# Blockwise attention and a cosine feed-forward on one core: where the last blocks' weight differences are split, the banks of the last block, and an early table load

## The chip, the cores and the metric

The kernel runs on one core of a Trainium2 chip. The metric is device microseconds of an execution. TensorE (PE) multiplies, and PEld in the profile is its loading of weights; VectorE (DVE), ScalarE (ACT) and GpSimd (POOL) compute; SyncE (SP) issues all transfers, in one fixed order.

## The reference

```
q, k, v: (8, 8, 576, 64) float32;  w_in: (512, 2048);  w_out: (2048, 512)
for every head and every chunk of 64 positions:
    s = q_c @ k_c.T / 8;  s = s - max(s);  a = exp(s);  a = a / (sum(a) + 1e-9);  out_c = a @ v_c
x = out, positions by heads: (4608, 512)
h = x @ w_in;  g = h * cos(h);  result = g @ w_out          # (4608, 512) float32
```

## The kernel before, in words

Tokens are worked in nine tiles of 512. Every large product is made in three passes of a rounded type (float32r): an operand is split into a high part (a rounding copy) and a low part (the operand less its high part), and high by high, high by low and low by high are summed in one bank of the accumulator memory. `copy_by` (L337) is the copy and `two_by` (L343) the subtraction; they run on the engine that the order names, so most splits of the whole kernel share the lines L339, L341 and L345. All matmuls have line 324 and all loads line 321.

The program does not issue its work directly. `piece` (L1076) records each step with its engine, an estimated length and what it waits for; at the end `in_order` (L283) issues all of them in the order of the list `RANK` (one place for each recorded piece), and the pieces in the list `ELSEWHERE` go to their other engine (ScalarE's copies to VectorE, VectorE's subtractions to GpSimd). On each engine and on SyncE the work runs strictly in that order. A reader can't see from the list which piece is where, so the places that matter are told in words below.

The start: `early` (L1137) makes the scores of four head pairs of tile 0; the first pair's maximum is negated and its exponentials are made chunk by chunk (L514), for the others the maximum is subtracted first (L506) and the exponential follows (L578). VectorE takes the maxima (L502), sums (L594) and inverses (L598, L599).

The middle: from tile 3 on, tiles go in pairs (a "unit"). The hidden layer of two tiles is made with seven products of half blocks instead of eight, named A11, S3, S2, A12, A22, S1, S4, whose weight operands (`combo`) were stored in the device's main memory (HBM) and are streamed in four rooms. Two of the units also make differences of w_out's blocks, `differences_of_w` (L1684): for each of eight pairs of row blocks it forms four differences V1 to V4, splits them into high and low parts on chip, and stores both parts in `diffs`.

The last unit: `last_pair` (L1781) makes the hidden layer of the last two tiles for eight pairs k. In a pair, the product S4 needs two adds on VectorE (`add_c`, `add_b`), which need the copy of S3's bank (`copy_d`). After S4 comes a chain of integer part (L972), turn (L975), sine (L979), product (L982), rounding copy and low part, before the pair's own block products. Sums of g's quarters (Z1 to Z4 and Z22) go to `sums` in HBM. Then `last_blocks` (L1911) makes the remaining products of the output layer: Z1 by V1, Z2 by V2, Z3 by V3, Z4 by a quarter of w_out itself, Z22 by V4, each in four groups kk, for tile i = 0 and 1. For each group it loads the difference (`w_load`), loads two sums into a room of a ring (`g_load`), splits the sums (`parts_of_g`), and multiplies (`block_part`). A sub-block of 128 by 256 of one group is six matmuls of 256 columns. Results are copied out of the banks X, Y, Z into the rows A to D, added to, and stored by `store_block`.

```
ring: K_ROOMS[0][0], K_ROOMS[1][0] (pair 6's), K_ROOMS[0][1], K_ROOMS[1][1] (pair 7's), two rooms of x
```

Of the kernel before, what the change touches and what calls it, by code (L numbers as in the profile page):

```python
# [20 lines left out]
P = 128  # L21
# [70 lines left out]
    35, 32, 38, 44, 48, 41, 16, 56, 60, 65, 66, 54, 72, 79, 81, 78, 74, 84, 90, 94, 87, 82, 93, 96, 98, 97, 101,  # L92
    110, 113, 116, 107, 109, 114, 120, 126, 131, 115, 135, 137, 142, 134, 123, 138, 147, 150, 149, 144, 162, 171,
    177, 156, 146, 159, 165, 168, 188, 180, 196, 200, 203, 193, 178, 201, 209, 214, 216, 227, 231, 237, 240, 222,
    233, 248, 250, 253, 262, 244, 266, 271, 273, 265, 257, 268, 270, 278, 277, 267, 280, 285, 287, 282, 288, 297,
    321, 328, 305, 300, 310, 316, 324, 331, 327, 335, 338, 344, 336, 322, 341, 351, 354, 347, 339, 353, 355, 356,
    362, 352, 365, 367, 368, 366, 364, 377, 380, 385, 378, 384, 388, 390, 397, 394, 386, 402, 406, 413, 403, 400,
    405, 412, 417, 420, 416, 422, 430, 441, 421, 409, 425, 438, 448, 447, 435, 453, 457, 460, 455, 442, 458, 462,
    467, 0, 14, 1, 2, 3, 4, 5, 7, 8, 11, 6, 12, 17, 20, 9, 19, 24, 27, 15, 26, 30, 10, 13, 22, 25, 28, 31, 36, 42,
    18, 23, 34, 39, 46, 45, 49, 29, 37, 43, 50, 53, 52, 59, 40, 47, 55, 63, 69, 61, 68, 51, 58, 62, 70, 75, 71,  # L100
    77, 21, 33, 64, 163, 92, 100, 105, 173, 95, 130, 172, 175, 111, 133, 186, 191, 179, 176, 205, 197, 183, 187,
    192, 211, 215, 219, 198, 207, 199, 204, 213, 221, 220, 224, 226, 228, 236, 241, 234, 238, 246, 255, 259, 252,
    256, 57, 67, 73, 80, 85, 88, 91, 99, 103, 106, 76, 83, 86, 89, 104, 108, 112, 117, 125, 127, 102, 119, 122,
    128, 136, 140, 148, 132, 129, 118, 124, 121, 141, 145, 151, 154, 167, 169, 143, 155, 158, 139, 152, 153, 157,
    160, 174, 182, 194, 170, 161, 166, 181, 164, 184, 190, 195, 208, 223, 225, 189, 202, 185, 210, 206, 212, 217,
    230, 245, 249, 260, 218, 243, 232, 229, 239, 235, 242, 247, 263, 269, 276, 264, 307, 258, 254, 251, 261, 274,
    283, 286, 289, 295, 299, 284, 279, 275, 272, 281, 291, 293, 296, 301, 304, 309, 302, 290, 294, 292, 298, 320,
    475, 308, 477, 314, 317, 303, 306, 535, 312, 313, 315, 318, 325, 329, 311, 332, 330, 319, 340, 333, 342, 346,
    349, 357, 360, 350, 334, 326, 323, 337, 359, 363, 369, 372, 375, 383, 361, 343, 348, 358, 345, 371, 374, 381,
    387, 398, 401, 382, 373, 370, 379, 376, 391, 395, 404, 407, 410, 414, 399, 389, 396, 424, 393, 419, 423, 428,  # L110
    432, 444, 449, 440, 450, 464, 446, 468, 470, 486, 491, 483, 493, 499, 507, 511, 518, 521, 528, 529, 542, 583,
    554, 545, 547, 561, 563, 568, 574, 548, 552, 565, 567, 576, 582, 586, 591, 609, 607, 601, 608, 612, 621, 625,
    629, 590, 597, 604, 619, 623, 627, 633, 660, 642, 649, 418, 415, 427, 411, 408, 426, 429, 433, 436, 439, 443,
    445, 437, 434, 451, 431, 452, 461, 465, 471, 480, 490, 466, 485, 454, 482, 463, 473, 481, 484, 488, 492, 494,
    487, 498, 513, 456, 459, 497, 503, 508, 515, 520, 526, 500, 495, 502, 512, 517, 504, 510, 514, 524, 527, 536,
    525, 519, 509, 506, 522, 531, 537, 539, 550, 553, 556, 530, 569, 558, 540, 546, 541, 559, 562, 566, 578, 581,
    560, 555, 551, 549, 544, 570, 572, 575, 585, 598, 602, 580, 573, 599, 577, 571, 587, 588, 595, 605, 630, 634,
    610, 606, 589, 603, 596, 615, 626, 628, 632, 635, 641, 624, 618, 617, 622, 614, 646, 648, 639, 644, 640, 643,
    638, 645, 647, 653, 656, 661, 668, 671, 637, 654, 657, 665, 667, 658, 664, 666, 669, 672, 676, 670, 681, 659,
    652, 663, 680, 684, 686, 688, 696, 701, 685, 697, 678, 694, 683, 692, 703, 705, 708, 714, 719, 702, 734, 691,  # L120
    722, 731, 712, 715, 720, 723, 738, 751, 713, 748, 753, 729, 711, 724, 730, 733, 737, 757, 760, 725, 392, 479,
    476, 478, 474, 533, 592, 532, 469, 472, 489, 496, 534, 501, 505, 516, 523, 593, 538, 543, 557, 564, 594, 579,
    584, 600, 611, 613, 616, 620, 631, 636, 651, 655, 662, 674, 677, 689, 693, 706, 650, 728, 690, 699, 726, 750,
    727, 673, 675, 679, 704, 687, 739, 700, 732, 695, 710, 716, 721, 709, 717, 682, 698, 707, 735, 743, 766, 740,
    747, 741, 745, 718, 772, 779, 778, 785, 820, 947, 857, 916, 834, 933, 986, 997, 1008, 764, 809, 842, 825, 758,
    815, 811, 762, 771, 783, 829, 791, 824, 831, 839, 902, 946, 777, 884, 943, 736, 742, 744, 746, 752, 770, 763,
# [2264 lines left out]
```

## Time and profile before

| | us |
|---|---|
| median of 3 runs (lowest, highest) | 782.38 (779.45, 783.24) |
| the profiled execution | 779.57 |
| its span, first to last instruction | 777.8 |
| PE busy in the span | 763.4 |
| DVE / ACT / POOL busy | 637.9 / 442.8 / 256.5 |

The granted clock of TensorE is 0.999 of full speed over the span. 184.59 MB move on the queue of the kernel's transfers. Times in the rows count from the span's start.

### The profile page before, as it was taken

To read this page: it belongs to the slowest core of one execution; us is meant where nothing else is said; L and a number is where in the kernel's file an instruction comes from. 1 tells how busy PE (TensorE), PEld (TensorE's weight loads), DVE (VectorE), ACT (ScalarE), POOL (GpSimd) and SP (SyncE) were. 2 spreads that over 40 slices of the span, in tenths; PEclk is the share of its full clock that TensorE was granted. 3 is DMA by queue.
4 is the path that set the end of the run, shared out by engine and by line. 5 is a ranking of instruction groups with operands and counts; after the bars stand their busy time and mean duration, and the time that the engine had idled before them with its cause. 6 is when DMAs were issued, how large, how long until landed. Compare 5 with 4: busy or idle time off the path is not lost.

```text
span 777.8 us, 16133 instructions
## 1 busy us (share of the span) xinstructions
PE 763.4 (98%) x6100; PEld 675.5 (87%) x6100; DVE 637.9 (82%) x1120; ACT 442.8 (57%) x811; POOL 256.5 (33%) x241
## 2 busy tenths in 40 slices
PE   7999999999999999999999999999999999999997
PEld 6888888888999988888888888888888889888997
DVE  5997889988999988987887878987788676688664
ACT  5998887366874547555644256454625366556222
POOL 2344125665443145341102345222123243433011
PEclk9999999999999999999999999999999999999999
DMA  9991922099959655897636737668743457999994
GB/s 336 409 419 44 350 83 82 23 333 329 340 188 303 210 195 204 266 316 234 215 108 236 254 114 267 214 217 305 244 139 123 162 173 253 295 284 376 374 382 148
DMA packets 100109, 185.61 MB, mean 239 GB/s; under 512 B 9408, under 2 KB 44224, under 8 KB 100032
## 3 DMA queue, kind: packets, MB, share of 16 engines
q1 hardware_dynamic: 100032, 184.59, 68.3%
q8 instruction: 48, 0.79, 0.4%
q14 instruction: 29, 0.24, 0.1%
HBM read 132.12 MB, written 52.43 MB: 237 GB/s over the span
## 4 chain that ended last, share of the span: by engine, by line
PE 88%; DVE 5%; DMA 3%; ACT 2%; issue 1%; SPq 1%; POOL 0%; ACTq 0%; DVEq 0%; POOLq 0%
PE acc L324 43%; PE h L324 33%; PE a L324 12%; DMA w_in<-combo 1%; DMA kt<-in_kT_dram 1%; DMA diffs<-w_in 1%; SPq L321 1%; DMA w_in<-sums 1%; DVE w_in L975 0%; DVE w_in L982 0%; ACT g_hi L341 0%; PE a L1202 0%; DVE g_lo L345 0%; DVE w_in L345 0%; ACT e L514 0%
## 5 line engine op out<-in xcount | busy, mean ns | idle before, releaser
L324 PE MATMUL acc<-w_out,g_hi 128*128 128x512 f32 (+1 forms) x992 | 281.6, 368 | 0.3 <-DVE g_hi L339 0.2
L324 PE MATMUL h<-x,w_in 128*128 128x512 f32 (+1 forms) x960 | 226.0, 364 | 0.2 <-DVE g L725 0.2
L324 PEld LDWEIGHTS acc<-w_out,g_hi 128*128 128x128 f32 x992 | 180.8, 189 | 23.9 <-DVE g_hi L339 0.4
L324 PEld LDWEIGHTS h<-x,w_in 128*128 128x128 f32 x960 | 170.9, 189 | 22.7 <-DVE x L687 0.5
L324 PE MATMUL acc<-w_out,g_lo 128*128 128x512 f32 (+1 forms) x496 | 181.5, 366 | 0.9 <-DVE g_lo L345 0.9
L345 POOL TENSOR_TENSOR g_lo<-g,g_hi 128x512 fp32r<-128x512 f32 x41 | 57.3, 1397 | 155.6 <-DVE g_hi L339 60.0
L324 PEld LDWEIGHTS acc<-w_out,g_lo 128*128 128x128 f32 x496 | 93.9, 189 | 12.9 <-DVE g_lo L345 1.3
L324 PE MATMUL h<-w_in,w_in 128*128 128x512 f32 (+1 forms) x384 | 98.3, 354 | 1.1 <-DMA w_in<-combo 0.9
L324 PEld LDWEIGHTS h<-w_in,w_in 128*128 128x128 f32 x384 | 65.8, 190 | 10.1 <-issue 1.0
L341 ACT CAST g_hi<-w_in 128x512 fp32r<-128x512 f32 x46 | 28.4, 619 | 54.3 <-PE acc L324 28.9
L345 DVE TENSOR_TENSOR g_lo<-w_in,g_hi 128x512 fp32r<-128x512 f32 x56 | 38.3, 689 | 18.8 <-ACT g_hi L341 16.7
L979 ACT ACTIVATE w_in<-w_in 128x512 f32<-128x512 f32 x64 | 39.3, 627 | 22.9 <-DVE w_in L975 22.8
L345 POOL TENSOR_TENSOR g_lo<-w_in,g_hi 128x512 fp32r<-128x512 f32 x16 | 20.9, 1310 | 63.4 <-DVE g_hi L339 30.3
L324 PE MATMUL a<-x,w_in 128*128 128x512 f32 (+1 forms) x192 | 41.1, 353 | 0.4 <-ACT g_hi L341 0.4
L324 PE MATMUL a<-w_in,w_in 128*128 128x512 f32 (+1 forms) x192 | 41.0, 353 | 0.0
L972 ACT ACTIVATE w_in<-w_in 128x512 int32<-128x512 f32 x32 | 20.1, 628 | 31.2 <-DVE w_in L969 25.8
L341 ACT CAST g_hi<-g 128x512 fp32r<-128x512 f32 x44 | 27.1, 618 | 18.1 <-PE acc L324 12.4
L324 PEld LDWEIGHTS a<-x,w_in 128*128 128x128 f32 x192 | 32.9, 190 | 4.6 <-ACT g_hi L341 0.7
L324 PEld LDWEIGHTS a<-w_in,w_in 128*128 128x128 f32 x192 | 32.9, 190 | 3.9
L966 ACT COPY a<-h 128x512 f32<-128x512 f32 x28 | 16.0, 573 | 33.7 <-PE h L324 33.6
L975 DVE SCALAR_TENSOR_TENSOR w_in<-w_in,h 128x512 f32<-128x512 int32 x32 | 21.9, 683 | 15.8 <-ACT w_in L972 13.3
L345 DVE TENSOR_TENSOR g_lo<-g,g_hi 128x512 fp32r<-128x512 f32 x43 | 32.1, 749 | 1.3 <-ACT g_hi L341 0.8
(250 smaller groups left out, 1483.1 us busy)
## 6 DMA issues: line engine op xcount, KB each, us to landing
w_in<-combo SPq DMA_DIRECT2D x84, 512.0 KB, 5.2
combo<-w_in SPq DMA_DIRECT2D x56, 256.0 KB, 5.0
w_in<-combo SPq DMA_DIRECT2D x56, 256.0 KB, 5.2
w_in<-sums SPq DMA_DIRECT2D x40, 256.0 KB, 6.2
qt<-in_qT_dram SPq DMA_DIRECT2D x36, 256.0 KB, 5.3
kt<-in_kT_dram SPq DMA_DIRECT2D x36, 256.0 KB, 5.5
w_in<-in_w_in_dram SPq DMA_DIRECT2D x16, 512.0 KB, 9.5
w_out<-in_w_out_dram SPq DMA_DIRECT2D x16, 512.0 KB, 9.6
```

What stands on the lines that cost most here:

```text
L321: kept(nc.sync.dma_start(out=out, in_=in_))
L324: kept(nc.tensor.matmul(*args, **kw))
L341: kept(nc.scalar.copy(out=out, in_=in_))
L345: kept(eng.tensor_tensor(out, a, b, op=op))
L966: kept(nc.scalar.copy(out=out, in_=in_))
L972: kept(nc.scalar.activation(g.bitcast(I32), h, AF.Identity, bias=0.25, scale=0.5 / math.pi))
L975: kept(nc.vector.scalar_tensor_tensor(g, g.bitcast(I32), -2.0 * math.pi, h, op0=ALU.mult, op1=ALU.add))
L979: kept(nc.scalar.activation(g, g, AF.Sin, bias=0.5 * math.pi))
```

## The change

- `differences_of_w` no longer splits: it stores the four differences as they are, two stores a call instead of four, and `diffs` has half the size.
- `w_load` loads a difference (256 KB instead of 512) into the low half of a room, and then two new pieces split it there: `high` (ScalarE, or VectorE) and `low` (VectorE, or GpSimd).
- The rooms are others: the two tiles of exponentials and a pair of `vt` tiles first, then the four streaming rooms, then nine rooms of x. Three more rooms of x join the ring of g's split parts (`g_where`). The ring of loaded sums begins with the two g tiles, so every later group moves up one room.
- Tile 1's last product (Z22 by V4) goes into a bank "W" of its own for each half, the banks that Z had; row D takes a copy of X after P7, and each half of W is added to it on VectorE.
- `added_to` stores its two halves as two pieces with places of their own. The copies of C wait for those of B.
- A memset and one exponential of a 128 by 1 tile stand at the start of the program.

```diff
+    table = const.tile([P, 1], F32, name="table")
+    kept(nc.vector.memset(table, 0.0))
+    kept(nc.scalar.activation(table, table, AF.Exp))
...
     def g_high(t, fc, g, by):
-        g_parts[t, fc] = g_room(t == FAST)
+        g_parts[t, fc] = g_where[t, fc]() if g_where.get((t, fc)) else g_room(t == FAST)
...
-    diffs = [hbm.tile([P, 4, 2, 2, HALF], F32, name=f"diffs{kk}") for kk in range(KK)]
+    diffs = [hbm.tile([P, 4, 2, HALF], F32, name=f"diffs{kk}") for kk in range(KK)]
...
-            block_bank[key] = bank(*{"X": ("acc", 2 * i), "Z": ("acc", 2 * i + 1), "Y": ("a", i)}[name])
+            block_bank[key] = bank(*{"X": ("acc", 2 * i), "Z": ("acc", 2 * i + 1), "Y": ("a", i), "W": ("acc", 2 * i + 1)}[name])
...
-        o, first = block_of(name, i)
-        cols = slice(sub * HALF, (sub + 1) * HALF)
+        o, first = block_of(name, sub if name == "W" else i)
+        cols = slice(0, HALF) if name == "W" else slice(sub * HALF, (sub + 1) * HALF)
...
-        lo = piece(DVE, 1.7, taken, a, port=True, other=(POOL, 3.0, False))
-        stores = diffs_of[k] = []
-        for i in range(2):
-            h = piece(ACT, 0.62, lambda by, i=i: high(i, by), lo, *stores, other=(DVE, 0.45, True))
-            stores.append(piece(SP, 0.65, lambda i=i: keep(i, 0), h, lag=2.0))
-            lo = piece(DVE, 0.69, lambda by, i=i: low(i, by), h, port=True, other=(POOL, 1.3, False))
-            stores.append(piece(SP, 0.65, lambda i=i: keep(i, 1), lo, lag=2.0))
+        a = piece(DVE, 1.7, taken, a, port=True, other=(POOL, 3.0, False))
+        diffs_of[k] = [piece(SP, 0.5, lambda i=i: keep(i), a, lag=2.0) for i in range(2)]
...
+                hi, lo = w_room[kk, j] = room()
+                load(lo.bitcast(F32), diffs[kk][:, j].rearrange("p n q -> p (n q)"))
+            def high(by):
+                hi, lo = w_room[kk, j]
+                copy_by(by, hi, lo.bitcast(F32))
+            def low(by):
+                hi, lo = w_room[kk, j]
+                two_by(by, lo, lo.bitcast(F32), hi.bitcast(F32), ALU.subtract)
+            p = piece(SP, 0.65, go, *free, *(p for k in (2 * kk, 2 * kk + 1) for p in diffs_of[k]), lag=2.0)
+            p = piece(ACT, 0.62, high, p, other=(DVE, 0.45, True))
+            here["w", kk, j] = piece(DVE, 0.69, low, p, port=True, other=(POOL, 1.3, False))
+        ring = deque([(lambda: [g_tile(), g_tile()], list(g_free))])
...
-            piece(SP, 0.65, lambda: store_block(t + i, rows[i, name], m, half), p, lag=2.0)
+            for s in range(2):
+                piece(SP, 0.6, lambda s=s: store_block(t + i, rows[i, name], m, half, [s]), p, lag=2.0)
...
+        gate["P4", 1] = one_done
+        three = copied(1, "D", "X", "P7")
...
+                if i:
+                    def go(sub=sub):
+                        ...
+                        o = block_bank["W", sub][:, :HALF].rearrange("p (k n) -> p n k", n=2)
+                        kept(nc.vector.tensor_tensor(r, r, o, op=ALU.add))
+                    p = piece(DVE, 0.42, go, *last, three)
+                    piece(SP, 0.6, lambda sub=sub: store_block(t + 1, rows[1, "D"], 1, 0, [sub]), p, lag=2.0)
+                    continue
```

RANK and ELSEWHERE are new lists (3216 pieces instead of 3225). Their first ten places hold the same pieces; of TensorE's 906 pieces 707 have another place on their engine. The places that the prediction speaks of:

| where | old order | new order |
|---|---|---|
| VectorE, after head pair 1's subtraction | inverse for pair 0, then maximum of pair 2 | maximum of pair 2, then inverse for pair 0 |
| ScalarE in pair 7, after A11 | copies b, d; a rounding of g; copy c; integer part of g1 | copies b, c; a rounding of g; rounding of V2's block 3, of V1's block 1; integer part of g1; copy d |
| TensorE in pair 7, between A22 and S4 | five block products of three matmuls | four |
| TensorE in pair 7, after S4 | five such products, then four that need g1 and g2, then four that need g3 and g4 | the same numbers |
| room of V2's block 3 | x's room of A12 (second) | x's room of A11 (first) |
| ScalarE between pair 7's last sine and the rounding of g3, g4 | nothing | roundings of V3's blocks 2 and 3 |
| SyncE at the very end | D's first half of tile 1, both halves of B (tile 0), D's second half | D's first half of tile 1, D's second half, one half of A (tile 0) |

Five of the 16 new subtractions are on GpSimd. V1's blocks 0 and 2 are loaded and split before the last pair.

## Rows read from the trace of the kernel before

**Rows 1.** The page, section 1: engine, busy us, share, instructions.

```profile
PE 763.4 (98%) x6100; PEld 675.5 (87%) x6100; DVE 637.9 (82%) x1120; ACT 442.8 (57%) x811; POOL 256.5 (33%) x241
```

**Rows 2.** By stretches: length, busy PE, PEld, DVE, ACT, POOL; PEclk, DMA share, GB/s.

```profile
20.00:640.00 620.00, 619.16 (x4898) 542.63 (x4898) 530.89 (x933) 369.44 (x670) 214.05 (x194) 1.00 0.64 222
...
700.00:726.00 26.00, 23.62 (x163) 21.13 (x162) 20.34 (x38) 13.18 (x23) 6.73 (x7) 1.00 1.03 369
726.00:771.00 45.00, 45.00 (x403) 44.84 (x403) 30.01 (x50) 13.45 (x22) 6.39 (x5) 1.00 0.86 316
```

**Rows 3.** The chain that ended last: start us, us, what.

```profile
761.41 10.07 PE acc L324 x90
```

**Rows 4.** TensorE in order of time: start, us, line, tiles, count, idle before.

```profile
671.16 0.28 PE L324 MATMUL acc<-w_out,g_lo 128*128 128x256 f32 x1
672.32 1.53 PE L324 MATMUL h<-w_in,w_in 128*128 128x512 f32 x6 [0.89 <-DMA w_in<-combo]
...
711.93 0.49 PE L324 MATMUL acc<-w_out,g_hi 128*128 128x256 f32 x2
713.02 0.38 PE L324 MATMUL acc<-w_out,g_lo 128*128 128x256 f32 x1 [0.60 <-DVE g_lo L345]
...
721.85 0.28 PE L324 MATMUL a<-w_in,g_lo 128*128 128x256 f32 x1
722.88 0.49 PE L324 MATMUL a<-w_in,g_hi 128*128 128x256 f32 x2 [0.76 <-ACT g_hi L341]
723.61 0.38 PE L324 MATMUL a<-w_in,g_lo 128*128 128x256 f32 x1 [0.24 <-DVE g_lo L345]
...
771.19 0.28 PE L324 MATMUL acc<-x,g_lo 128*128 128x256 f32 x1
771.93 0.49 PE L324 MATMUL acc<-x,g_hi 128*128 128x256 f32 x2 [0.46 <-ACT vt L341]
772.26 0.28 PE L324 MATMUL acc<-x,g_lo 128*128 128x256 f32 x1
```

**Rows 5.** ScalarE, then VectorE, in order of time in the first 12 us.

```profile
6.40 1.28 ACT L514 ACT_TABLE_LOAD   x1 [6.40 <-DVE m L509]
7.70 0.32 ACT L514 ACTIVATE e<-acc,m 128x64 f32<-128x64 f32 x1
...
8.95 0.69 DVE L506 TENSOR_TENSOR e<-acc,m 128x512 f32<-128x512 f32 x1
10.21 0.17 DVE L598 TENSOR_SCALAR z<-z 128x8 f32<-128x8 f32 x1 [0.57 <-ACT e L514]
...
10.54 0.64 DVE L502 TENSOR_REDUCE m<-acc 128x8 f32<-128x512 f32 x1
```

**Rows 6.** Pair 7 in order of time: S3, S2's start, S4's start.

```profile
700.09 1.46 PE L324 MATMUL a<-w_in,w_in 128*128 128x512 f32 x6
701.76 0.48 PE L324 MATMUL h<-w_in,w_in 128*128 128x512 f32 x1 [0.21 <-ACT h L966]
...
708.72 1.46 PE L324 MATMUL h<-w_in,w_in 128*128 128x512 f32 x6
```

**Rows 7.** Groups by line: splits of differences; count, busy us, mean ns, idle before.

```profile
L341 ACT CAST w_in<-w_in 128x512 fp32r<-128x512 f32 x14 | 8.5, 615 | 3.5 <-POOL w_in L345 2.5 <-issue 0.7 <-DMA diffs<-w_in 0.3
...
L345 DVE TENSOR_TENSOR w_in<-w_in,w_in 128x512 fp32r<-128x512 f32 (+1 forms) x14 | 11.2, 800 | 0.1
```

**Rows 8.** Landing: the loads of diffs from 690 us, then issues from 640 us.

```profile
DMA to landing us min/median/max: 5.2/7.1/8.6
...
w_in<-sums SPq DMA_DIRECT2D x40, 256.0 KB, 6.2
```

**Rows 9.** The end: VectorE's last copy and SyncE's last issues, in order of time.

```profile
772.97 0.42 DVE L339 COPY vt<-acc 128x256 f32<-128x256 f32 x1 [3.01 <-PE acc L324]
...
773.26 1.25 SPq L1072 DMA_DIRECT2D out_dram<-w  x2
774.61 0.55 SPq L1072 DMA_DIRECT2D out_dram<-vt  x1
```

More of the change, by code (lines that the diff above doesn't have):

```diff
@@ L984, in attention_then_cos_ffn @@
     rounds = [3]
+    g_where = {}
     def g_room(roomy):
@@ L1483, in parts_of_g @@
         pool.append((t, fc))
+        g_where[t, fc] = g_where.get(back)
         h = piece(
@@ L1914, in last_blocks, with x_flat @@
         n_loads = len(stream_room)
-        w_free = deque(
-            [("kept", stream_room[i], used_by[i]) for i in range(n_loads - len(KEPT_ROOMS), n_loads)]
-            + [("x", (j, part), [x_used[j]]) for j in (A11, S3, S2, A12, S1, A22) for part in range(2)]
-        )
+        x_rooms = [(j, part) for j in (A11, S3, S2, A12, S1, A22, S4) for part in range(2)]
+        def x_flat(j, part, dtype):
+            name = (wide_rooms + list(X_ROOMS))[2 * j + part]
+            if isinstance(name, str):
+                return x_named(name, dtype).rearrange("p n q -> p (n q)")
+            return w_in_room(name, dtype)[:, PAD : PAD + 2 * TOK]
@@ L1919, in last_blocks @@
+        n_w = 4 * KK - len(w_free)
+        for j, part in x_rooms[:n_w]:
+            w_free.append((lambda j=j, part=part: in_halves_of(x_flat(j, part, F32R)), [x_used[j]]))
+        for j, part in x_rooms[n_w : n_w + 3]:
+            key = "extra", (j, part)
+            g_pool.append(key)
+            spent[key] = [x_used[j]]
+            g_where[key] = lambda j=j, part=part: in_halves_of(x_flat(j, part, F32R))
         here = {}
         def w_load(kk, j):
-            kind, room, free = w_free.popleft()
+            room, free = w_free.popleft()
@@ L1942, in last_blocks @@
-        ring.append((("x", (S4, 1)), [x_used[S4]]))
+                room = K_ROOMS[i][n]
+                ring.append((lambda room=room: in_halves_of(w_in_room(room, F32)[:, PAD : PAD + 2 * TOK]), k_users[i, NPAIR - 2 + n]))
+        for j, part in x_rooms[n_w + 3 :]:
+            ring.append((lambda j=j, part=part: in_halves_of(x_flat(j, part, F32)), [x_used[j]]))
         v = {}
@@ L1975, in w_parts_at @@
                 return [w_at(2 * (2 * kk + n) + 1, 1, part) for part in range(2)]
-            return [lambda part=part: w_block[kk, d][:, n, part] for part in range(2)]
+            return [lambda part=part: w_room[kk, d][part][:, n * HALF : (n + 1) * HALF] for part in range(2)]
         def products(group, *deps):
@@ L2034, in last_blocks @@
         five = {i: copied(i, "B", "Y", "P5") for i in range(2)}
-        two = {i: copied(i, "C", "X", "P6") for i in range(2)}
+        two = {i: copied(i, "C", "X", "P6", *five.values()) for i in range(2)}
         for i in range(2):
@@ L2057, in last_blocks @@
             for sub in range(2):
+                last = [p for n, p in enumerate(block_pieces["P4", i]) if n % 2 == sub]
+                if i:
+                    def go(sub=sub):
+                        cols = slice(sub * HALF, (sub + 1) * HALF)
+                        r = rows[1, "D"][:, cols].rearrange("p (n k) -> p n k", n=2)
+                        o = block_bank["W", sub][:, :HALF].rearrange("p (k n) -> p n k", n=2)
[3 more added lines that the diff above has]
+                    continue
                 def go(by, i=i, sub=sub):
```

72 lines of the change are left out of this document (27 added, 45 removed), and 369 rows, old and new, of tables (ELSEWHERE, RANK).

## The prediction

> **What bounds the kernel now.** The engine table of the page comes first: TensorE is busy 763.4 us of a span of 777.8, so all other engines together can give back 14.4 us [rows 1]. The table by stretches says where those lie: from 20 to 640 us TensorE lacks 0.84 us in 620, from 700 to 726 it lacks 2.38 in 26, from 726 to 771 nothing [rows 2]. So whatever the change takes off VectorE, ScalarE or the queues in the middle is worth nothing by itself; it can only matter in the first 20 us, between 640 and 726, and in the last 7. The transfers are at 369 GB/s with a busy share of 1.03 between 700 and 726 [rows 2]: there TensorE's neighbours wait for data. Last I read the matmul starts around the idle times, because an engine that restarts loses more than its idle time shows. The chain of waits has 90 matmuls of 256 columns in 10.07 us, 0.112 us each [rows 3]; a start that comes later than 0.11 us a matmul is a loss. By that measure the stretch from 640 on loses 1.05 us at 672.3 (671.16 to 672.32, one matmul: 1.16 less 0.11), where a matmul waits for a `combo` load; 0.87 at 713.0; 0.92 and 0.51 at 722.9 and 723.6; 0.63 at 771.9 (771.19 to 771.93) [rows 4].
>
> **The change part by part.**
>
> *Table of exponentials at the start.* The load takes 1.28 us, from 6.40 to 7.68, and the first exponential follows at 7.70 [rows 5]; ScalarE was idle before it. It goes, and the bound on the gain is 1.28. But VectorE, which feeds TensorE here, lost less: it was free at 9.64 (8.95 + 0.69), waited 0.57 for the exponentials of head pair 0, and began the maximum of head pair 2 at 10.54 [rows 5]. The new order puts that maximum first, so VectorE runs on. Behind it VectorE is the queue that all later steps stand in, so I take its 0.57 us and not 1.28; the lower end is 0, if the weights' arrival sets the first hidden products. The added memset and activation stand where both engines have nothing else.
> The Trainium skill (ScalarE: Activation LUTs, What ACT_TABLE_LOAD costs) adds about 1.38 us of draining to a switch, 2.66 in all. Here the exponential starts 0.02 us after the load, so the row decides; by the rule the gain could reach 2.66, and the sum would be up to 1.4 us better.
>
> *Differences of w_out unsplit.* Removed from the two middle units: 16 rounding copies, 16 low parts and 16 of 32 stores of 256 KB. They lie beside a TensorE that is full [rows 2]: 0, between -0.5 and +0.5. Added in the last 80 us: 16 copies of 0.62 us, most on ScalarE, and 16 subtractions of 0.69 to 0.8 us [rows 7]. VectorE is busy 20.3 of 26 us between 700 and 726 and 30.0 of 45 after [rows 2]; five of the subtractions go to GpSimd, two blocks are loaded and split before the last pair, so some 8 us of VectorE work meet some 20 us of free time. As work it fits. As a wait it need not: the copies stand in ScalarE's fixed order, and whatever is behind one waits until its load has landed.
> The place where that costs is the last pair. The new order has on ScalarE, after the copy of bank c: the rounding of V2's block 3, that of V1's block 1, the first link of g1, and only then the copy of S3's bank, which both adds ahead of S4 need. V2's block 3 goes into a room that product A11 of this pair frees, at 700.09 [rows 6], so its load can't be issued sooner. From landing to the end of that copy are four steps of some 0.6 us, 2.3 together; the copy must be done 1.3 us (two adds of 0.68) before S4 may start. S4 started at 708.72 [rows 6]; in the new order it has one block product (0.34) fewer ahead of it, so it wants to start at 708.38. Nothing is lost if the load lands by 704.8, that is 4.7 us after issue; every us later is a us of TensorE. Loads of 256 KB take 6.2 us here, those of 512 KB from `diffs` 5.2 to 8.6 [rows 8]. Half the bytes of `diffs` are gone, so I expect less than 6.2 and take 5.5: **+0.8**, bounds 0 and +3.9 (8.6).
> The Trainium skill (DMA: Bandwidth & Descriptors, Anatomy of one DMA) gives a transfer 2 us plus its bytes at 436 GB/s: by it 256 KB land in 2.6 us, nothing waits, and the sum is 0.8 better. The rows show more than twice that under load, so I don't go by it.
>
> *Rooms of the last blocks.* Before, Z1's third group went into the room of the last pair itself, free only once that pair's sums were taken; the two waits at 722.9 and 723.6 follow: 0.92 + 0.51 [rows 4]. Now the first group takes the two g tiles, every later one moves up a room, and the third gets a room of the pair before the last. **-1.43**, bounds 0 and -1.43. Three more g rooms remove the wait of a rounding for old products, but those waits were on ScalarE only. The wait at 713.0 (0.87) is the last pair's own chain from S4 to its low part; both orders put five and then four block products behind S4, so it stays: 0, between -1.2 (the 2.38 us of idle time from 700 to 726 less the 0.21, 0.76 and 0.24 told of elsewhere [rows 2, 4, 6]) and +0.5.
>
> *The end.* The last block has two banks, so the matmul at 771.93 no longer waits for the copy of the first half of the same bank: 0.63 by its start, and 0.11 more at its successor (0.33 between them for two matmuls): **-0.74** [rows 4]. The last copy ran 772.97 to 773.39, but its store began at 774.61, because two transfers of rows B stood in between [rows 9]: 1.22 us. In the new order nothing stands before that store, but one transfer of rows A (half of 1.25) is issued after it and ends last: 0.03 + 0.62 us instead of 1.22, **-0.57**. Bounds for both: -0.74 and -1.93. The landing after the last issue (2.64 to 777.8) stays.
>
> *The new order as a whole.* RANK is rewritten: of 906 pieces on TensorE 707 have another place. In the middle the old one loses 0.84 us, so it can hardly gain and may lose: 0, bounds -0.5 and +2. Between 640 and 705 the old one lost 1.05 + 0.38 us (six matmuls from 700.09, 1.30 us, and the next at 701.76) [rows 6] on a load and a copy that came just too late; under another order I expect half of that: **-0.7**, bounds -1.4 and +1.4.
>
> **Sum:** -0.57 + 0.8 - 1.43 - 0.74 - 0.57 - 0.7 = -3.2 us. The profiled execution took 779.57 (its span and 1.8 us around it), so one like it would take 776.4. That execution is 2.8 us below the median of the runs, 782.38, which lie from 779.45 to 783.24; I let the changed kernel's runs scatter alike and forecast 782.4 - 3.2 = **779.2**.
>
> **Rivals.** *More is won:* the table's full 1.28, the last pair's copies in time (0), all waits from 640 to 705 gone (1.43), and the end's full 1.93: -1.28 - 1.43 - 1.43 - 1.93 = -6.1, 776.3. For it: most of these are bounded by rows, not guessed; against: every one must come off. *It doesn't do what it says:* the first hidden products wait for weights as before, the last pair gives back what the rooms save, another order costs what it saves, and only -0.7 to -1.3 of the end remain: 781.1 to 781.7. For it: TensorE is 98% busy, and stalls that a fixed order removes come back elsewhere. *Slower:* the roundings of w blocks in ScalarE's order. There are three bunches of them (before the last pair's S4, after its last sine, and among the first blocks), and each block in them is issued late on a queue whose transfers land after 5.2 to 8.6 us. Taken at the first one's slack for all, it decides from 6.0 us on, where 1.33 us at each eat the -4.0 of the rest; at 6.9 us it is 6.6 - 4.0, 785.0, and at 8.6 us 11.7 - 4.0, 790.1. For it: loads of 7.1 us now [rows 8], and g's rounding behind each; against: half the bytes, and the second and third bunch have about 6 us from issue to use in the new order, more than the first.
>
> **How the numbers follow.** Forecast 0.47, more won 0.22, nothing won 0.20, slower 0.11. The forecast's own range is 777.5 to 781; with the rivals the range is 775.3 to 783.2, which leaves out the late-load case and the far end of the first. I count 0.5% as about what a measurement of this kernel can tell from no change: below 778.5 is faster, above 786.3 slower. The first rival and a third of the forecast (with a scatter of 2 us) make faster 0.39; same 0.52; slower 0.09.
>
> **What would show it.** Right: no table load at 6.4 us and the maximum of head pair 2 at about 9.7; no wait of TensorE for a rounding some 5 us after the last pair; the last two sub-blocks without a gap; the last store within 0.1 us of its add and one store after it. Wrong: a stall ahead of S4 longer than 1.5 us or none; ScalarE waiting for `diffs` in the blocks; TensorE idle by more than 2 us between 20 and 640; head products starting at 19.2 as before.

## The result and the profile after

| | before | after |
|---|---|---|
| median of 7 runs, us (lowest, highest) | 782.38 (779.45, 784.96) | 789.07 (786.71, 790.67) |
| after / before, 95% interval | | 1.008 (1.0055 to 1.0104) |
| the profiled execution, us | 779.57 | 789.2 |
| its span, us | 777.8 | 787.4 |

The change makes the kernel slower, by 0.8%; 779.2 had been forecast, and 789.07 is outside the range. The medians differ by 6.7 us, the two profiled executions by 9.6, all of it within the span: before's was among its fastest. What follows reads these two executions, so its microseconds are larger than those of the medians.

The first view is the engine table of the page and the table by stretches (length; busy PE, PEld, DVE, ACT, POOL; PEclk, DMA share, GB/s):

```profile
PE 767.6 (97%) x6100; PEld 679.3 (86%) x6100; DVE 648.0 (82%) x1121; ACT 442.2 (56%) x814; POOL 257.3 (33%) x240
```

```profile
20.00:640.00 620.00, 612.66 (x4856) 536.76 (x4857) 520.99 (x905) 352.99 (x642) 208.43 (x188) 1.00 0.62 214
...
700.00:726.00 26.00, 23.01 (x129) 20.53 (x130) 21.18 (x38) 16.25 (x29) 6.60 (x7) 0.94 0.87 280
726.00:771.00 45.00, 44.18 (x385) 43.37 (x385) 35.68 (x58) 20.85 (x38) 12.90 (x9) 1.00 0.84 286
```

TensorE had lost 0.84 us between 20 and 640 us; now it loses 7.34 there and runs 42 matmuls fewer in the same time [rows 2]. The amount of transfers is not the reason: their share fell from 0.64 to 0.62. To place the loss I counted the matmul work done (all 6100 matmuls, each at its pitch in undisturbed rows) and compared the times at which both kernels began the same amount:

```
before at, us             55    105   181   228   303   631   692   718   758   end
after later by, us        0.0   2.1   5.5   7.9   9.9   8.9   8.1   10.6  10.9  9.6
```

So nothing is won in the head, 9.9 us are lost between 55 and 303 and 1.0 of them won back by 631 (8.9 in all, where run 1's expectation has 8.3), 0.7 is won before the last pair, 2.5 lost in it, 0.3 lost in the blocks and 1.4 won at the end. The next view is TensorE in order of time (start, us, line, tiles, count, idle time before and its releaser) around the places where starts come late:

```profile
59.99 0.38 PE L323 MATMUL acc<-w_out,g_lo 128*128 128x512 f32 x1
62.25 1.28 PE L323 MATMUL a<-pts,vt 64*64 64x64 f32 x64 [1.88 <-DMA vt<-in_v_dram]
...
156.24 0.33 PE L323 MATMUL a<-pts,vt 64*64 64x64 f32 x4
158.09 1.15 PE L323 MATMUL a<-pts,vt 64*64 64x64 f32 x60 [1.52 <-DVE pts L641]
...
215.73 0.38 PE L323 MATMUL acc<-w_out,g_lo 128*128 128x512 f32 x1
217.73 0.24 PE L323 MATMUL h<-kt,qt 64*64 64x64 f32 x1 [1.62 <-DMA kt<-in_kT_dram]
...
720.01 0.28 PE L323 MATMUL acc<-w_out,g_lo 128*128 128x256 f32 x1
722.05 0.49 PE L323 MATMUL acc<-w_out,g_hi 128*128 128x256 f32 x2 [1.76 <-ACT g_hi L340]
723.20 0.58 PE L323 MATMUL acc<-w_out,g_lo 128*128 128x256 f32 x1 [0.66 <-DVE g_lo L344]
...
782.80 0.28 PE L323 MATMUL acc<-x,g_lo 128*128 128x256 f32 x1
```

By start to start less the matmul's own pitch the first costs 2.04 us (a load of v), the second 1.72 (transposes of the exponentials), the third, with its successors until 220, 2.6 (keys), the last two 1.93 and 0.93. Two more in the front, 0.56 at 266 and 1.18 at 289, and 1.7 us at a lower clock behind the second stall (the last section) make up most of what is lost there.

The second stall shows how an order does this. VectorE and GpSimd in order of time, after first, then VectorE's same four subtractions before:

```profile
149.53 3.59 DVE L344 TENSOR_TENSOR w_in<-half,w_in 128x256 fp32r<-128x256 f32 x4
...
153.75 2.23 DVE L641 STREAM_TRANSPOSE pts<-e 32x256 f32<-32x256 f32 x5
...
156.73 1.22 DVE L641 STREAM_TRANSPOSE pts<-e 32x256 f32<-32x256 f32 x3
```

```profile
150.10 1.32 POOL L344 TENSOR_TENSOR g_lo<-g,g_hi 128x512 fp32r<-128x512 f32 x1 [2.23 <-ACT g_hi L340]
151.38 2.88 POOL L344 TENSOR_TENSOR w<-w_in 128x512 f32<-128x512 f32 x2
```

```profile
157.54 1.39 DVE L345 TENSOR_TENSOR w_in<-half,w_in 128x256 fp32r<-128x256 f32 x4
```

The new list has them on VectorE beside a low part and sums on GpSimd: 3.59 us instead of 1.39, and the transposes that a matmul waits for stand behind them. The first two take 0.42 us each as before, the last two 1.50, and each of these ends 0.29 us after the GpSimd instruction beside it. The Trainium skill (SBUF — State Buffer, SBUF: two separate sides) says that the two engines' shared port pair is an exclusive lock, taken for a whole instruction, so that the other engine blocks; these rows agree, at 2.20 us for four small subtractions.

The third is SyncE's fixed order. After (first fence) the loads of queries and keys for the next tile are issued behind streamed operands; before (second) they had gone out 11 to 13 us earlier, when 5.5 us of the lateness were already there:

```profile
204.51 0.43 SPq L320 DMA_DIRECT2D qt<-in_qT_dram  x1
...
212.49 0.57 SPq L320 DMA_DIRECT2D kt<-in_kT_dram  x1
```

```profile
191.92 0.43 SPq L321 DMA_DIRECT2D qt<-in_qT_dram  x1
...
201.08 0.33 SPq L321 DMA_DIRECT2D kt<-in_kT_dram  x1
```

### The profile page after: what moved, and what is told of

Same layout as the page of the kernel before. It is cut to its first block, busy times and chain, and to the rows that moved or that the text cites. A ratio compares the mean times of both kernels' runs of the same rounds, so it can differ in the third digit from the quotient of the medians.

```text
span 787.4 us, 16036 instructions
## 1 busy us (share of the span) xinstructions
PE 767.6 (97%) x6100; PEld 679.3 (86%) x6100; DVE 648.0 (82%) x1121; ACT 442.2 (56%) x814; POOL 257.3 (33%) x240
## 4 chain that ended last, share of the span: by engine, by line
PE 80%; DMA 8%; DVE 7%; issue 2%; SPq 1%; ACT 1%; POOL 1%; ACTq 0%; DVEq 0%
PE acc L323 37%; PE h L323 31%; PE a L323 12%; DMA kt<-in_kT_dram 2%; DMA vt<-in_v_dram 2%; DMA w_in<-combo 2%; DVE w_in L344 1%; DMA w_in<-sums 1%; DMA sums<-qt 1%; SPq L320 1%; DMA sums<-w_in 1%; DVE g_lo L344 1%; DVE w L344 0%; DVE pts L641 0%; DVE e L344 0%
## 5 line engine op out<-in xcount | busy, mean ns | idle before, releaser
L344 POOL TENSOR_TENSOR g_lo<-g,g_hi 128x512 fp32r<-128x512 f32 x38 | 52.5, 1382 | 209.2 <-DVE g_hi L338 119.0
L340 ACT CAST g_hi<-g 128x512 fp32r<-128x512 f32 x48 | 29.6, 617 | 34.4 <-PE acc L323 23.2
L344 DVE TENSOR_TENSOR g_lo<-g,g_hi 128x512 fp32r<-128x512 f32 x49 | 37.5, 767 | 4.5 <-ACT g_hi L340 3.8
L344 DVE TENSOR_TENSOR g_lo<-w_in,g_hi 128x512 fp32r<-128x512 f32 x41 | 31.3, 768 | 6.7 <-ACT g_hi L340 5.6
L340 ACT CAST g_hi<-w_in 128x512 fp32r<-128x512 f32 x33 | 20.3, 617 | 24.7 <-PE acc L323 15.7
L974 ACT ACTIVATE w_in<-h 128x512 int32<-128x512 f32 x32 | 19.1, 596 | 26.2 <-PE h L323 25.9
```

The lines of the kernel that those rows point to most:

```text
L340: kept(nc.scalar.copy(out=out, in_=in_))
L344: kept(eng.tensor_tensor(out, a, b, op=op))
L974: kept(nc.scalar.activation(g.bitcast(I32), h, AF.Identity, bias=0.25, scale=0.5 / math.pi))
```

## The experiments

Two theories stood at first. **Order:** the new places of the front lose the time, the edits little. **Edits:** the table load, the rooms or the last pair lose it, and the front merely follows. Each run has its own runs of before beside it on the same chip; all ratios are to those. How far a run stands behind or ahead of before at a time is by the count of matmuls above. What the order lists give in numbers is told below in words; diffs of them name recorded pieces by number.

**1. The old order in front, all edits kept.** Places up to the last unit's first product from the old list (without the pieces that the change removes), the new order behind. The old `ELSEWHERE` goes with the old places: 187 pieces of the front change their engine. "Order" below means both lists.

```diff
-RANK = new
+RANK = old up to the last unit's first product (place 2422), new behind it; ELSEWHERE likewise
```

> All edits of the change, but the old order up to the first product of the last unit (place 2422) and the new order from there. By the amount of matmul work begun, the changed kernel stands 8.3 us behind the old one at 640 us. Theory (the places of the pieces lose it, not the edits): no stall of TensorE over 0.6 us before 640, the profiled execution 8.3 us shorter than the changed kernel's 789.2, so 780.9, ratio to the kernel before 1.002. Rival (the edits in the middle lose it: fewer stores and roundings shift transfers into each other): it stays at 786 to 789, ratio 1.008.

0.9988 (0.9974 to 1.0003), 780.43 us. The order theory holds: against 1.008 the front's order is worth 0.92%, 7.2 us. Its "no stall over 0.6 us" does not: 1.10 us at 60 stay. With the front's loss gone, all edits and the last unit's new order together are worth nothing that can be measured.

**2. Three moves in the new order**, one for each of the first three stalls.

```diff
 SyncE:   ... store 379, load 345 ...      (345 was ahead of 379)
+SyncE:   loads of queries and keys (832, 833) ahead of the stream (724)
+GpSimd: 700 (four subtractions); VectorE: 702 (a sum of two blocks)    (each the other's)
```

> The changed kernel with its own order but for three places: the loads of the third tile's queries and keys (8 transfers) stand behind an output store again; the queries and keys of tile 4 (8 transfers) stand ahead of the streamed operands again; one step of four subtractions goes back from VectorE to GpSimd, and a sum of two blocks from GpSimd to VectorE. Theory (each long stall has one misplaced step): the stalls at 60 (2.05 us), at 156 with the half clock behind it (3.3) and at 216 to 220 (2.6) go, 8.0 in all: 781.2 in the profile, ratio 1.000. Rival (a dense order is late everywhere, and a stall that is taken away comes back at the next late step): at most 3 us are won, 786, ratio 1.005.

1.0053 (1.0033 to 1.0072). The stall at 156 shrinks to 0.41 us of idle time and the one at 216 goes, the one at 60 stays, and a wait for a streamed operand turns up elsewhere, 1.53 us at 263 where it was 0.39: 1.8 us behind before at 105, 5.8 at 303. The local moves give back a third of the loss, as the rival had it.

**3. One swap in the old order:** load 345 ahead of store 379, as in the new one.

```diff
-SyncE: 379, 345
+SyncE: 345, 379
```

> The kernel before with one swap among its 3225 pieces: the 8 loads of the third tile's queries and keys are issued ahead of an output store instead of behind it. Theory (they then share the engines with the two value loads that TensorE needs at 60 us): a stall of some 2 us at 60 us and nothing else, 781.6 in the profile instead of 779.57, ratio 1.0026. Rival (the stall of the changed kernel comes from the order of the weights before it, which end 1 us later there): no stall, 779.6, ratio 1.000; in between, 0.5 to 1 us.

1.0005 (0.9992 to 1.0017), and the product of v starts at 61.97 without a wait; v lands 5.2 us after its issue, before's took 6.5. That swap is not what makes v late; the cause of the stall at 60 was open.

**4. The last pair mended, on run 1.** In run 1 ScalarE's roundings of V2's block 1 stood in the way of g, as they do after (ScalarE in order of time, after):

```profile
717.42 0.62 ACT L340 CAST w_in<-w_in 128x512 fp32r<-128x512 f32 x1 [1.94 <-DMA w_in<-diffs]
717.95 0.62 ACT L981 ACTIVATE w_in<-w_in 128x512 f32<-128x512 f32 x1
...
721.38 0.62 ACT L340 CAST g_hi<-w_in 128x512 fp32r<-128x512 f32 x1 [0.27 <-DVE w_in L984]
```

A sine has its input, but stands behind a rounding whose load lands 1.94 us late; g's rounding follows, and TensorE waits at 720 and again at 722.

```diff
-ScalarE, VectorE: V2 block 1's rounding and low part (3012, 3013) ahead of g's chain
+ScalarE, VectorE: 3012, 3013 behind g's last rounding (2942)
+ScalarE: copy of S3's bank (2904) ahead of the integer part (2888)
```

> As the first of these kernels, and in the last pair the rounding of V2's block 1 (ScalarE) and its low part (GpSimd) stand behind g's last rounding instead of ahead of the turn of g1, and the copy of S3's bank ahead of a rounding of g. Theory (ScalarE waits 1.94 us for that block's load, with the chain of g1 to g4 behind it): the stall of 1.93 + 0.93 at 720 and the half clock behind it (together 2.9 us of progress) shrink to the 0.9 that the old order had there: 2 to 2.9 us less than the first kernel, 778.0 to 778.9 in the profile. Rival (the chain is bound by VectorE or by S4 itself): at most 0.5 less.

0.9991 (0.9977 to 1.0005). The stall at 720 goes, nothing of the 2 us that the theory had is won, and the next in line takes its place: the same engine now waits for other loads, and g's block products come 1.96 us late at 727.07. ScalarE of this kernel:

```profile
724.20 0.62 ACT L332 CAST x<-x 128x512 fp32r<-128x512 f32 x1 [2.45 <-DMA x<-diffs]
726.40 1.26 ACT L332 CAST g_hi<-w_in 128x512 fp32r<-128x512 f32 x2 [1.58 <-DMA w_in<-sums]
```

**5 to 7. The table's tile.** The stall at 60 stayed in run 1 with the old order (1.10 us), so an edit makes it. Between 45 and 51 us the queue is full and a load of 512 KB follows every 1.28 us, where it was 1.235. In run 1 the only edit that had acted by then is the table's; its tile is allocated ahead of all others and moves every later tile by 32 bytes a partition. The edit alone in before (run 6), and a tile of 64 bytes in after (5) and in before (7):

```diff
+    table = const.tile([P, 1], F32, name="table")                 # run 6, before's order
+    table = const.tile([P, 16], F32, name="table")[:, :1]         # runs 5 (after) and 7 (before)
```

> The changed kernel, with the small table tile widened from 1 to 16 columns (only the first is used). In the compiled program the 1-column tile stands ahead of all large tiles and moves them by 32 bytes of each partition (w_in's first block from byte 5760 to 5792); with 16 columns it moves them by 64 (5824). In all runs with the tile the 512 KB loads between 30 and 50 us follow each other every 1.275 us (396 to 410 GB/s from 20 to 50 us), in those without it every 1.235 (404 to 421). Theory (the 32 bytes slow the transfers): the old spacing of 1.235 us comes back, the values land 1.2 us sooner and the stall at 60 us shrinks from 2.04 to 0.5 to 1.2; the stalls for keys at 216 to 220 get shorter too; 786 to 788 in the profile instead of 789.2. Rival (the halved store of differences, or another order of the loads, sets the rate): 1.275 us and 2 us of stall as before, 789.

> The kernel before with nothing added but the table load at its start as in the change (1 column). Theory (32 bytes): the loads follow each other every 1.275 us, TensorE is 0.5 to 1 us ahead at 50 us because the table is loaded early, and loses 1 to 1.5 us at 60 us to values that land late; in all 779.3 to 780.5 in the profile against 779.57, ratio 0.9995 to 1.002. Rival (the rate comes from other edits): 1.235 us, no stall at 60, the 0.57 us of the prediction won: 779.0.

> The kernel before with the table load at its start, the tile 16 columns wide. Theory (32 bytes): spacing of 1.235 us; TensorE 0.5 to 1 us ahead at 50 us, and at most 0.5 of that lost at 60 us, where the old kernel had no wait: 778.8 to 779.3, ratio 0.999. Rival (early loads of the exponentials' table move the loads of values): as the run with 1 column.

1.0106 (1.0083 to 1.0128), 1.0003 (0.9983 to 1.0023) and 0.9999 (0.9979 to 1.0018). The edit alone brings the slow loads (1.28) and a wait of 1.31 us at 60 into the old order, so this edit is the cause; whether by its tile's place or by its early load of the table, run 9 tells. A shift of 64 bytes does the same as 32 (1.28 in both runs), and the theory that only an odd 32 hurts falls.

**8. All mends in one:** run 4, the wide tile, and a store of rows A ahead of the very last ones.

```diff
+    table = const.tile([P, 16], F32, name="table")[:, :1]
+SyncE: store 2958 (rows A, tile 0) ahead of the last stores
```

> As the kernel with the old order in front and the two roundings of the last pair moved back, with the table 16 columns wide and the store of rows A (tile 0) issued ahead of the last two stores instead of behind them. Theory: the stall at 60 us (1.55) shrinks below 0.7, that at 725 us (2.12, a rounding that waits for loaded sums) to 1 to 1.5 because sums land sooner, and 0.6 us go after the last matmul: 777 to 778 in the profile, ratio to the kernel before 0.996 to 0.998. Rival (the last stretch is bound by when rooms come free, not by transfers): only the 0.9 at 60 and 0.6 at the end, 779.6 less what the scatter gives, ratio 0.998 to 0.999.

0.9977 (0.9961 to 0.9992), 779.77 us: faster than before by 0.2%, though its interval overlaps run 4's. What it has beyond run 4 is the store at the end; the wide tile is no cure (run 7).

**9 to 11. The tile in a pool behind all others**, so that nothing moves: before with the table (9), after (10), run 8 (11).

```diff
+    last = ctx.enter_context(tc.tile_pool(name="last", bufs=1))
-    table = const.tile([P, 1], F32, name="table")
+    table = last.tile([P, 1], F32, name="table")
```

> The kernel before with the table load at its start, the 1-column tile in a pool of its own behind all others, so that every other tile keeps its address (w_in's first block at byte 5760). With the tile in front, 32 or 64 bytes wide, the 512 KB loads followed each other every 1.275 us; without it every 1.235. Theory (a shift of the large tiles by 32 or by 64 bytes slows the loads alike): 1.235 us, the head's 0.3 to 0.5 us kept, no wait over 0.4 us for values at 60 us: 778.8 to 779.4 in the profile against 779.57, ratio 0.9985 to 1.0. Rival (what is done in the first us slows the loads, wherever the tile lies): 1.275 us and a wait of 1.1 to 1.3 us at 60, ratio 1.000 to 1.002.

> The changed kernel with the table's tile behind all others. Theory (addresses): spacing 1.235 us, the stall at 60 us shrinks from 2.04 to 0.8 to 1.2 (the new order wants the values 0.8 us sooner than the old one, which had no wait), the others stay within 0.5 us: 787.5 to 788.3 in the profile, ratio 1.005 to 1.008. Rival: 1.275 and 2.0 us of stall, 789, ratio 1.009.

> As the best kernel so far (old order in front, two roundings of the last pair moved back, the store of rows A issued earlier), with the table's tile behind all others. Theory (addresses): nothing over 0.4 us lost at 60 us instead of 0.98, loads of sums a little sooner in the last 60 us: 778.3 to 779.5 in the profile instead of 780.56, ratio to the kernel before 0.995 to 0.997. Rival: 0.9977 as that kernel.

1.0012 (0.9992 to 1.0033), 1.0064 (1.0039 to 1.0089) and 0.9974 (0.9959 to 0.9988). SyncE's issues of the same loads, after and then run 9, and TensorE's product of v, run 6, then run 9, then run 10:

```profile
48.49 0.33 SPq L320 DMA_DIRECT2D w_out<-in_w_out_dram  x1
49.77 0.33 SPq L320 DMA_DIRECT2D w_in<-in_w_in_dram  x1
```

```profile
46.16 0.33 SPq L322 DMA_DIRECT2D w_in<-in_w_in_dram  x1
47.40 0.33 SPq L322 DMA_DIRECT2D w_out<-in_w_out_dram  x1
```

```profile
61.92 1.24 PE L324 MATMUL a<-pts,vt 64*64 64x64 f32 x64 [1.31 <-DMA vt<-in_v_dram]
```

```profile
60.81 1.16 PE L325 MATMUL a<-pts,vt 64*64 64x64 f32 x64
```

```profile
60.36 1.28 PE L324 MATMUL a<-pts,vt 64*64 64x64 f32 x64 [1.03 <-ACT half L410]
```

Intervals of 1.28 us against 1.24, and in the old order the wait is gone: the place is the cause, not the early load. In the new order 1.03 us of the 1.88 stay. The old order's waits with the tile in front (runs 1, 4, 6, 7 and 8) are 0.83 to 1.40 us; in the medians of the old order what the place costs can't be told from nothing (1.0003 and 1.0012 overlap), and after's two intervals overlap too. Run 10 still loses 1.51 us at 156 (line below), 0.95 and 0.67 on keys at 213 to 215, and goes from 1.1 us ahead at 55 to 5.3 behind at 303, where run 11, with the old order in front, is 0.2 ahead: the order. Its TensorE:

```profile
156.19 1.15 PE L324 MATMUL a<-pts,vt 64*64 64x64 f32 x60 [1.51 <-DVE pts L642]
...
213.46 0.24 PE L324 MATMUL h<-kt,qt 64*64 64x64 f32 x1 [0.95 <-DMA kt<-in_kT_dram]
```

**12. The reverse of run 1:** before's code in the new order up to the last unit (both lists).

```diff
-RANK = old
+RANK = new up to the last unit (the 16 roundings and stores that it lacks get places by guess)
```

> None of the edits: the kernel before with the places of the new order up to the last unit's first product, and the old ones behind it. Theory (the places alone lose it): the stalls at 156, 216 to 220, 266 and 289 stand as in the changed kernel, the one at 60 is smaller because the table's tile is not there; 6.5 to 8 us behind at 640 and 786 to 787.5 in the profile, ratio 1.008 to 1.010. Rival (places and edits lose it together): under 3 us behind at 640, ratio below 1.004.

1.0462 (1.0434 to 1.0489). Up to 330 us it has run 10's stalls (1.72 at 154.6, 1.18 at 284) and is 4.9 us behind at 303, without any of the edits, as the order theory has it. Behind that the guessed places lose far more than the 1.008 to 1.010 expected, first 6.04 us at once:

```profile
337.77 2.50 PE L317 MATMUL h<-x,w_in 128*128 128x512 f32 x5 [6.04 <-DVE g L975]
```

So from 330 on this run says nothing on the question.

**13 and 14. Shifts of 128 and 512 bytes** in before, one run each.

```diff
+    table = const.tile([P, 32], F32, name="table")[:, :1]     # 14: [P, 128]
```

> The kernel before with the table load, the tile ahead of all others and 32 columns wide: the large tiles move by 128 bytes (w_in's first block from byte 5760, which is 45 times 128, to 5888). Moved by 32 and by 64 bytes the 512 KB loads follow each other every 1.275 us, unmoved every 1.235. Theory (a tile must begin on a multiple of 128 bytes): 1.235 us, no wait over 0.4 us for values at 60 us. Rival (any move breaks it, since the old place is a multiple of 512 plus 128): 1.275 us and a wait of about 1 us.

> As the run before, 128 columns wide: the large tiles move by 512 bytes. Both theories of that run: 1.235 us. A third (the tile in front of the weights slows the loads whatever its size): 1.275 us.

Loads every 1.24 us in both (414 and 409 GB/s from 20 to 50 us), and no wait over 0.15 us at the product of v. SyncE, run 13:

```profile
47.22 0.33 SPq L321 DMA_DIRECT2D w_out<-in_w_out_dram  x1
48.45 0.33 SPq L321 DMA_DIRECT2D w_in<-in_w_in_dram  x1
```

Slow at 32 and 64 bytes, fast at 0, 128 and 512: by these five places it is the place modulo 128 bytes that decides (96 was not run). The first block of w_in begins at byte 5760 of a partition before, 5792 after, 5824 with 64 bytes more and 5888 with 128. The Trainium skill (DMA: Bandwidth & Descriptors, How a descriptor splits into AXI transactions) says that an access may be shorter than 256 bytes but must start on a multiple of 256, so that a transfer that doesn't start there fetches bytes in vain. It speaks of what is read, and what moved here is where the loads write: 5760 is off by 128 and as fast as 5888, which is on, so for the written side the measurement puts the step at 128.

**15. The ring of loaded sums**, on run 11: x's rooms ahead of the last pair's, and four pieces moved, so that the sums land in time.

```diff
+            for j, part in x_rooms[n_w + 3 :] if n == 0 else ():
+                ring.append(...)            # ahead of the last pair's rooms
+SyncE: two loads of Z2's sums (3002, 3014) ahead of two stores
+V3's block 0: its rounding and low part (3026, 3064) later
```

> As the kernel with the old order in front, the repairs and the table's tile behind all others; and in the ring of loaded sums the two rooms of x come ahead of the last pair's rooms, the loads of Z2's first two groups are issued ahead of two stores of sums, and the rounding of V3's block 0 stands behind those of these sums on ScalarE. Theory (at 722.6 us TensorE waits 1.12 us for a rounding that waits 1.63 us for sums loaded into the last pair's room): that stall and the 0.5 behind it go, 776.2 to 776.9 in the profile instead of 777.85, ratio to the kernel before 0.995 to 0.997. Rival (transfers at 388 GB/s there are the bound): the wait comes back some us later, 777.8, ratio 0.9974.

0.997 (0.9955 to 0.9986). The wait that runs 4 and 11 have at 726 to 727 goes and others come back 10 to 14 us later, as the rival had it; run 15's TensorE:

```profile
736.50 0.38 PE L316 MATMUL acc<-x,g_lo 128*128 128x256 f32 x1 [0.86 <-POOL g_lo L337]
...
739.84 0.46 PE L316 MATMUL acc<-w_in,g_hi 128*128 128x256 f32 x2 [0.61 <-ACT vt L333]
```

**16. After's own order with the mends:** the tile last, the moves of queries and keys and of the split (run 2 without its swap), run 4's and run 8's.

```diff
+SyncE: 832, 833 ahead of 724; GpSimd 700, VectorE 702; 3012, 3013 behind 2942; 2904 ahead of 2888; 2958 earlier
+    table = last.tile([P, 1], F32, name="table")
```

> The changed kernel with its own order throughout, the table's tile behind all others, and three local repairs: the queries and keys of tile 4 ahead of the streamed operands, one step of subtractions on GpSimd and one of sums on VectorE (both as in the run with three moves), the two roundings of the last pair moved back and the store of rows A issued earlier. With the tile moved alone it took 784.97 in the profile, and lost 1.6 us at 156, 1.9 at 213, 1.3 at 285 and 2.5 to 3.7 at 715. Theory (four misplaced steps and the addresses are all that the change lost): 1.6 + 1.9 + 2.0 to 2.9 + 0.6 go, 778.0 to 778.9, ratio 0.996 to 0.999. Rival (this order is late everywhere): less than half of that comes, 781.5 to 783, ratio above 1.001.

1.0013 (0.9999 to 1.0027), 782.89 us. A few local moves and the tile's place bring 1.008 to 1.0013, with the rest of the new order kept; the theory wanted 0.996 to 0.999, which run 11 reaches with the same mends and the old order in front. From 55 to 631 us this run loses 3.0 us where run 10 lost 5.3 and run 11 0.2, so the moves give back less than half of what the order costs. What is left is a wait for v again (run 16's TensorE, below) and 1.17 at 283 in the front, and 2.23 at 727 in the last unit.

```profile
61.28 1.29 PE L316 MATMUL a<-pts,vt 64*64 64x64 f32 x64 [1.29 <-DMA vt<-in_v_dram]
```

The best versions are runs 11 and 15, 0.3% below before; their intervals overlap, so neither is the better one.

## Why the prediction was wrong, step by step

| step | predicted, us | measured, us |
|---|---|---|
| table, new order of the head (up to 55) | -0.57 | 0.0 |
| new order in the middle (55 to 631) | 0 (-0.5 to +2) | +8.9 |
| 631 to the last pair (692) | -0.7 | -0.7 |
| last pair (692 to 718) | +0.8 | +2.5 |
| rooms and blocks (718 to 758) | -1.43 | +0.3 |
| the end (from 758) | -1.31 | -1.4 |
| sum | -3.2 | +9.6 |

**The step that failed is the term "The new order as a whole", for the middle: "0, bounds -0.5 and +2".** It measured +8.9 (1.7 of it the lower clock behind the stall at 156, which run 10 doesn't show). The reasoning, that an order which loses only 0.84 us can hardly gain, was right, and the bound above was not one: nothing in the trace limits what 707 new places can lose, and the number of short slacks that the old order used up (v's load, the transposes, the keys) was never counted; nor were the pieces that change engine, of which four subtractions make the stall at 156. Run 1 shows that the order carries most of it, run 10 that it still loses 5.3 us there with the table's tile out of the way (run 11, old order: 0.2), run 12 that it does so without the edits, run 16 that two local moves there mend less than half of that. Which places cause the 3 us that remain in run 16 (waits for v, for transposes and for a low part) stays open. The prediction's own sign of this, TensorE idle by more than 2 us between 20 and 640, came. With +8.9 for this term the sum would have been +5.7.

**The table** was priced as an instruction of nothing and a gain of 0.57. The load does move; ScalarE and VectorE after:

```profile
0.73 1.28 ACT L352 ACT_TABLE_LOAD   x1 [0.73 <-PEq L2399]
```

```profile
9.12 0.69 DVE L504 TENSOR_REDUCE m<-acc 128x8 f32<-128x512 f32 x1
```

Head pair 2's maximum starts 1.42 us earlier than at 10.54 [rows 5]. What that is worth at 55 us can't be read from single traces: with the table, runs 1, 4, 6, 9, 10 and 11 stand 0.6, 0.9, 0.5, 0.2, 1.1 and 0.6 us ahead of before and after itself 0.0; without it, run 12 is 0.6 ahead and run 3, which starts as before does, 1.0 behind. A gain of 0.57 fits and isn't shown. After lacks it because TensorE stands idle for 1.24 us in its product of v, whose second load lands at 16.16 (run 10: 0.44 us, landing at 15.52):

```profile
16.31 0.21 PE L323 MATMUL acc<-pts,vt 64*64 64x64 f32 x1 [1.24 <-issue]
```

But its tile takes 32 bytes, and every queued load of 512 KB behind it follows 0.04 us later: between 20 and 50 us 404 GB/s were moved, with the tile last 413 and 414 (runs 9 and 10), and v at 60 us comes later for it. The tile had been costed at nothing because only its instructions' time was looked at. (One figure of the prediction is off: a gain of 2.66 would make its sum 2.1 us better than with the 0.57 taken, not 1.4.) How much of the 0.8% is the tile's stays open between nothing and 0.4% (1.008 and run 5's 1.0106 against run 10's 1.0064).

**The last pair.** S4 started only 0.28 us late (first rows): V2's block 3 landed 4.61 us after its issue where 5.5 had been taken, within the slack of 4.7 that had been worked out, and ScalarE waited 0.93 us for it (last row). So +0.8 was put at the wrong place; the mechanism, a rounding in ScalarE's fixed order waiting for a load of differences, is the one named in the rival that ends slower, with a 1.94 us wait for V2's block 1 beside S4, g's chain behind that, and the lower clock behind the stall.

```profile
716.66 0.28 PE L323 MATMUL acc<-w_out,g_lo 128*128 128x256 f32 x1
717.05 1.56 PE L323 MATMUL h<-w_in,w_in 128*128 128x512 f32 x6
```

```profile
713.38 0.62 ACT L340 CAST x<-x 128x512 fp32r<-128x512 f32 x1 [0.93 <-DMA x<-diffs]
```

What I missed is that the term must be looked up for every such rounding, not for the one nearest the end of the pair. But that rival was to lose by itself, and run 4 shows that its removal brings nothing that the runs can tell: another load is late next. The Trainium skill's 2.6 us for a load of 256 KB, which the prediction set aside, stands in that section under the path of transfers that GpSimd issues; these are SyncE's, and none of the 14 loads of differences landed in under 4.6.

**Rooms.** The two waits at 722.9 and 723.6 [rows 4] are gone, and new ones of 0.49, 0.32, 0.44 and 0.49 us stand at 736, 740, 750 and 751. The second rival, that stalls come back elsewhere, was right here, as it is in runs 2, 4 and 15.

**The end** is right in kind and in size, -1.4 for -1.31. The bank's wait of 0.63 us and the 0.11 behind it [rows 4] are gone, and from the start of the last matmul to the end of the span it takes 4.60 us (782.80 to 787.4) where it took 5.21 (772.59, three matmuls after the last row of [rows 4], to 777.8). Run 11, with the store of rows A moved up, takes 3.94, from the row below to 776.1.

```profile
772.16 0.28 PE L316 MATMUL acc<-x,g_lo 128*128 128x256 f32 x1
```

**631 to 692** came out at half of the old loss, as guessed; why it did was not looked into.

Not tried: the unsplit differences, the rooms and the two banks of the last blocks apart from each other. Run 1 bounds them together, with the table's shift and the last unit's new order in it: 0.9974 to 1.0003.

## What to carry to other kernels

Where one engine is full and everything runs in a fixed order, a rewritten order can be the largest edit of a change, whatever its few words call it, as it was here: count the loads and helper results that arrive with little to spare (the stalls here were up to 2 us), and give it a bound from those, not from the idle time of before. That count was not tried here. A tile allocated ahead of the others can cost through the places of all that come after it, though here only traces show it; allocate small ones last, or in steps that keep the large ones' alignment. A stall mended at one place is only a gain once the next one in the chain has been looked for.

## What the runs showed of the hardware

**A clock that falls after some stalls.** TensorE by single microseconds, after (length, busy PE, granted clock, DMA share, GB/s):

```profile
60.00:61.00 1.00, 0.37 (x2) 1.00 1.04 389
...
159.00:160.00 1.00, 1.00 (x18) 0.82 0.99 347
160.00:161.00 1.00, 1.00 (x3) 0.50 1.02 240
163.00:164.00 1.00, 1.00 (x6) 0.97 1.02 341
...
723.00:724.00 1.00, 0.80 (x4) 0.50 0.96 174
725.00:726.00 1.00, 1.00 (x7) 0.50 1.06 383
726.00:727.00 1.00, 1.00 (x9) 0.87 1.08 383
```

Behind the stalls at 156 and at 720 the clock stands at 0.50, the lower of its levels (1.2 GHz), until 163 and 726; full busy rows at 0.50 do half the work, 1.6 to 1.7 us lost each time beside the stall. After the longer stall at 60 (2.04 us) it stays at 1.00, and run 10's stall at 154 to 156 (1.51 us of idle time) brings no fall either. In run 5, the same program but for the tile's width, it is the other way round: the clock falls behind the stall at 60 (1.72 us of idle time) and not behind the one at 159 (1.54). What tells these apart isn't settled by these runs.

```profile
64.00:65.00 1.00, 1.00 (x4) 0.50 1.06 389
...
160.00:161.00 1.00, 1.00 (x19) 1.00 1.01 347
```

**A place in memory as a price.** Under a full queue the same 512 KB loads followed each other every 1.235 to 1.25 us with their tiles on a multiple of 128 bytes and every 1.28 off it, some 3% more (403 and 404 GB/s from 20 to 50 us in run 6 and after, 413 and 414 in runs 9 and 10). No other stretch was looked at.
